# Output products of two late blocks in the banks of h, and another order of the tail

## The chip, the cores and the metric

The kernel runs on one core of one Trainium2 chip. The metric is the time of the device for one execution, in microseconds (us); a kernel is run several times and the median counts. The kernel before takes 222.48 us in the median of three runs (222.0 to 222.53). A profile comes from one further look at the hardware: it lists every instruction with its start, its duration, and what it waited for.

The engines are named as the profile names them: PE is the matrix engine (TensorE), PEld its loads of weights, DVE the vector engine, ACT the scalar engine, POOL GpSimd, and SP the queue from which most transfers are issued.

## The reference

Two layers follow each other. The first is attention in which a query sees only the keys of its own cluster; the second works on each token by itself.

```python
q_assign = argmax(q_n @ c_n);  k_assign = argmax(k_n @ c_n)      # 16 clusters per head
scores = where(q_assign == k_assign, q @ k.T / sqrt(64), -1e9)
x = softmax(scores) @ v                       # 4 batches, 8 heads, 768 tokens, 64 per head
# x is put together to 3072 tokens of 512
h = x @ w_in                                  # 512 -> 1024
solu = h * softmax(h)
ln = (solu - mean(solu)) / sqrt(var(solu) + 1e-6) * g_ln
out = ln @ w_out                              # 1024 -> 512, float32
```

## The kernel before

**Work and names.** The 3072 tokens are 24 blocks of 128, numbered f = 0 to 23. Attention comes first in each batch (products S and V, exponentials E, normalisation N); a block of the second layer may start as soon as its tokens' attention is done. The last blocks thus form the tail of the kernel, in which nearly all work is that of the second layer. For a block f the steps are these, and they are the names in the order of the work:

- `h{f}.{f2}.{part}` (PE, line 772): the products x @ w_in; half f2 of the 1024 columns goes to the bank `hb[f2]`. Block 23 alone splits them by three and one slices of x, so that one product of each half remains to be done when the last slice of x is there.
- `hm{f}.{f2}` (DVE, line 782): reads the bank, writes -h to the tile w_st and takes the minimum. It frees the bank.
- `ex{f}` (ACT, line 798): exp with the sum over the row. `u{f}` (POOL or DVE, line 805): the product of both. Block 23 does these in two halves.
- `tu{f}` (SP, line 811): transposes u by a transfer. Blocks 22 and 23 do it on PE instead: `ptu{f}.{f2}` (line 759) puts half f2 into the first bank of sb1 or sb0, and `tu{f}.{f2}` copies it from there to `uT`, half 0 on ACT (line 768) and half 1 on DVE (line 766). This uT lies in the tile w_g, which held w_out and is free by then.
- `bn{f}.{f2}`, `as{f}`, `ag{f}` (DVE, lines 816, 835, 821 and 823): statistics of u, small sums, and the variance. `al{f}` (POOL, line 840): its power of -1/2, alpha.
- `y{f}.{part}` (PE, line 844): eight products of uT with w_out (centred beforehand) into the bank `mb`, two to a part. Parts 0 and 1 need the first half of uT, parts 2 and 3 the second. Block 23 makes two halves of 256 columns, one in the second bank of sb0, one in the bank ob.
- `sc{f}` (ACT or DVE, lines 856 and 858): alpha times the bank, into a tile y of which there are two. It frees `mb`. `ou{f}` (SP, for one half of block 23 ACT's queue; line 868): the transfer to memory.

**Order.** All steps stand in one list, `ORDER`, written out by hand, from which the program is made: each engine runs its own steps in the sequence of that list, one after the other, and a step that waits holds up what stands behind it on its engine. The table `AWAY` moves single steps to another engine. Semaphores between engines are set by the framework from the tiles that instructions read and write; the two banks of sb0 are one tile to it. `take` and `give` in a step's entry only assert that a bank is free in the list's sequence.

**What the steps around the change wait for.** `y21` stands behind `sc20`, since both use `mb`; `y22` behind `sc21`. In the list of before, `sc20` comes ahead of `ex23`, and `h23.1.1`, the last product of the last h, comes behind the eight products of `y20`. DVE makes `bn22` before and after it reads the first half of h of block 23. `sc{f}` writes a tile y, so it also waits until the transfer of block f - 2 has landed.

**The start.** Before the first transposes of q and k, PE runs seven products on zeros (`idle_products`, line 946), which fill the time until the first loads land.

Of the kernel before, what the change touches and what calls it, by code (L numbers as in the profile page):

```python
# [10 lines left out]
F32 = mybir.dt.float32  # L11
# [8 lines left out]
AWAY.update(dict.fromkeys("""  # L20
    ca0.0.1.1.0 ca0.2.0.1 ca1.0.0.1 ca3.1.1.0 ca3.2.0.1 cv0.0.1 cv0.1.0 cv0.2.1 cv1.2.0
    cv1.3.1 cv2.0.1 cv2.1.0 cv3.0.0 cv3.0.1 cv3.3.0 pl0.0.0.1 pl0.0.1.0 pl0.1.1.1 pl2.2.1.0
# [113 lines left out]
ptx23.0 h22.1.1 V95.0 ou16 sc18 V95.1 hm22.1 N40 tx23.0 ag20 tu19 y19.0 y19.1 y19.2 ptx23.1 y19.3  # L136
tu20 ou17 tu21 ou18 ex22.0 h23.0.0 h23.1.0 tx23.1 as22 bn21.0 bn21.1 ag21 u22.0 al20 sc19 h23.0.1
y20.0 y20.1 y20.2 y20.3 sc20 hm23.0 bn22.0 h23.1.1 ptu22.0 ptu22.1 bn22.1 hm23.1 tu22.1 tu22.0
ex23.0 ex23.1 ou19 y21.0 y21.1 y21.2 y21.3 ou20 u23.0 u23.1 ag22 as23 ptu23.0 ptu23.1 tu23.1
bn23.0 bn23.1 ag23 al21 sc21 ou21 tu23.0 y22.0 y22.1 y22.2 y22.3 y23.1.0 y23.1.1 y23.1.2 y23.1.3  # L140
y23.0.0 y23.0.1 y23.0.2 y23.0.3 al22 sc22 al23 sc23.0 sc23.1 ou23.1 ou22 ou23.0
""".split()
# [31 lines left out]
def kernel(  # L174
# [15 lines left out]
    P = 128  # L190
# [509 lines left out]
    def y_of(f, x=None):  # L700

        return mb[:] if x is None else (ob, sb[0][:, 1])[x][:, parts_of(f, x)]

# [58 lines left out]

    def keep_u(f, f2):
        dst = ff[f, "uT"][:, f2 * (n_fc // 2):(f2 + 1) * (n_fc // 2), :]
        if f2:
            nc.vector.tensor_copy(dst, tail_bank(f"tu{f}.{f2}"))
        else:
            nc.scalar.copy(dst, tail_bank(f"tu{f}.{f2}"))
# [82 lines left out]
    def f_scale(f, e, x=None):  # L851
        if (f, "o") not in ff:
            ff[f, "o"] = mo.tile([P, d_model], F32, name="y")
        c = parts_of(f, x)
        if e == "ACT":
            nc.scalar.activation(ff[f, "o"][:, c], y_of(f, x), Act.Copy, scale=ff[f, "alpha"][:])  # L856
        else:
            nc.vector.tensor_scalar(ff[f, "o"][:, c], y_of(f, x), scalar1=ff[f, "alpha"][:],  # L858
                                    scalar2=None, op0=Alu.mult)
# [83 lines left out]
    def idle_products():  # L943

        for _ in range(7):
            nc.tensor.matmul(sb[0][:, 0], idle[:, :P], idle)
# [235 lines left out]
    for f in range(n_f):  # L1182
# [63 lines left out]
        if f"tu{f}.0" in by_pe:  # L1246
            for f2 in range(n_ff2):
                turned(f"tu{f}.{f2}", (lambda f=f, f2=f2: turn_u_pe(f, f2)), 0.3, s,
                       "DVE" if f2 else "ACT", (lambda f=f, f2=f2: keep_u(f, f2)),
                       [us[min(f2, nhv - 1)]] + [f"ce{fc}" for fc in range(n_fc)])  # L1250
# [27 lines left out]
        free = [f"ou{f - 2}"] if f >= 2 else [f"ce{fc}" for fc in range(n_fc)]  # L1278
        if f < n_f - 1:
            e = on(f"sc{f}", "ACT")  # L1280
            add(f"sc{f}", e, 0.585 if e == "ACT" else 0.65, s + 5, (lambda f=f, e=e: f_scale(f, e)),
                [f"y{f}.3", f"al{f}"] + free, prior("sc{}", f), give="m")
            add(f"ou{f}", "SP", 0.5, s + 8, (lambda f=f: f_out(f, nc.sync)), [f"sc{f}"], move=0.76)
            continue
# [70 lines left out]
```

## Time and profile before

| | us |
|---|---|
| median of three runs | 222.48 (222.0 to 222.53) |
| span of the profiled execution, first to last instruction | 220.5 |
| PE busy | 211.4 |
| DVE busy | 185.7 |
| ACT busy | 192.8 |
| POOL busy | 158.8 |
| PE busy within the last 13.5 us | 9.63 |
| DVE busy within the last 13.5 us | 8.76 |

The page gives no time of the profiled execution beside its span, so the runs' median stands 2.0 above it for what lies around the span. In a row of the time line the first number is the start, the second the duration; "x8" says that eight like instructions stand together, and the duration runs from the first's start to the last's end. Products overlap: one begins before the one ahead of it has its result. Brackets hold the idle time of the engine ahead of the row and what ended it. In the chain of waits each piece is followed back from the last instruction to what released it.

### The profile page before, as it was taken

To read this page: it belongs to the slowest core of one execution; us is meant where nothing else is said; L and a number is where in the kernel's file an instruction comes from. 1 tells how busy PE (TensorE), PEld (TensorE's weight loads), DVE (VectorE), ACT (ScalarE), POOL (GpSimd) and SP (SyncE) were. 2 spreads that over 40 slices of the span, in tenths; PEclk is the share of its full clock that TensorE was granted. 3 is DMA by queue.
4 is the path that set the end of the run, shared out by engine and by line. 5 is a ranking of instruction groups with operands and counts; after the bars stand their busy time and mean duration, and the time that the engine had idled before them with its cause. 6 is when DMAs were issued, how large, how long until landed. Compare 5 with 4: busy or idle time off the path is not lost.

```text
span 220.5 us, 6292 instructions
## 1 busy us (share of the span) xinstructions
PE 211.4 (96%) x2401; PEld 148.9 (68%) x2431; DVE 185.7 (84%) x430; ACT 192.8 (87%) x245; POOL 158.8 (72%) x198
## 2 busy tenths in 40 slices
PE   7899999999999999999999999999999999999984
PEld 4567577677678776777677677666777767655442
DVE  3699979968999999896799999994888856989982
ACT  3799999999999998999999989999999888685362
POOL 3686969897898999549939997879889054456610
PEclk9999999999999999999999999999999999999999
DMA  5998999999999993999999981939584229777522
GB/s 199 394 402 259 189 175 300 126 154 259 164 154 169 190 188 62 174 248 210 153 225 162 180 184 38 171 92 209 151 173 90 72 64 168 154 120 170 163 94 100
DMA packets 120911, 38.33 MB, mean 174 GB/s; under 512 B 109993, under 2 KB 116401, under 8 KB 120881
## 3 DMA queue, kind: packets, MB, share of 16 engines
q1 hardware_dynamic: 120448, 37.40, 81.7%
q10 hardware_dynamic: 432, 0.52, 0.7%
q8 instruction: 19, 0.31, 0.6%
q14 instruction: 12, 0.09, 0.2%
HBM read 23.11 MB, written 6.29 MB: 133 GB/s over the span
## 4 chain that ended last, share of the span: by engine, by line
PE 72%; DVE 10%; DMA 6%; POOL 5%; issue 3%; ACT 2%; SPq 1%; DVEq 0%; ACTq 0%; POOLq 0%
PE sb L641 22%; PE hb L772 16%; PE mb L844 15%; PE ob L663 12%; DMA w_st<-in_moe_w_in_dram 4%; PE hb L470 3%; DMA raw<-in_q_dram 2%; DVE w_st L782 2%; PE hb L396 2%; DVE xt L421 2%; DVE bs L816 2%; POOL kbig L441 1%; PE mb L470 1%; POOL w_in_sb L580 1%; POOL v L556 1%
## 5 line engine op out<-in xcount | busy, mean ns | idle before, releaser
L651 ACT ACTIVATE e<-sb 128x1024 bf16<-128x1024 f32 x144 | 139.9, 1024 | 8.9 <-PE sb L641 8.1
L641 PE MATMUL sb<-qbig,kbig 80*128 80x256 bf16 (+3 forms) x648 | 83.8, 261 | 1.3 <-ACT e L651 1.0
L641 PEld LDWEIGHTS <-kbig 80*128 80x128 bf16 (+1 forms) x648 | 62.9, 119 | 25.4 <-issue 8.6
L805 POOL TENSOR_TENSOR u<-e_sb,w_st 128x1024 bf16<-128x1024 bf16 x21 | 45.1, 2145 | 20.0 <-ACT e_sb L798 13.3
L663 PEld LDWEIGHTS <-e 128*128 128x128 bf16 x1152 | 48.6, 97 | 10.4 <-DVE x L686 0.6
L663 PE MATMUL ob<-v,e 128*128 128x65 bf16 x1140 | 51.4, 193 | 0.2
L772 PE MATMUL hb<-w_in_sb,xT 128*128 128x512 bf16 x173 | 50.6, 379 | 0.9 <-POOL v L1323 0.3
L844 PE MATMUL mb<-w_out_c,uT 128*128 128x512 bf16 x165 | 45.5, 379 | 1.2 <-DVE y L858 0.4
L816 DVE BATCH_NORM_STATS2 bs<-u 128x6 f32<-128x512 bf16 x48 | 31.6, 680 | 1.1 <-POOL u L805 1.1
L798 ACT ACTIVATE e_sb<-w_st,nmax 128x1024 bf16<-128x1024 f32 (+1 forms) x25 | 27.8, 1113 | 3.2 <-DVE w_st L782 1.8
L439 POOL CAST qbig<-xt 64x768 bf16<-64x768 f32 (+1 forms) x31 | 25.7, 830 | 6.5 <-PE ob L663 2.7
L441 POOL TENSOR_SCALAR kbig<-xt 64x768 bf16<-64x768 f32 (+1 forms) x32 | 27.6, 865 | 2.4 <-DVE xt L409 0.8
L840 POOL TENSOR_TENSOR alpha<-var,halves 128x1 f32<-128x1 f32 x24 | 15.3, 638 | 12.6 <-DVE var L823 8.0
L421 DVE STREAM_TRANSPOSE xt<-raw 128x768 f32<-128x768 f32 x24 | 22.5, 959 | 0.1
L844 PEld LDWEIGHTS <-uT 128*128 128x128 bf16 x176 | 15.2, 97 | 10.2 <-issue 0.8
L772 PEld LDWEIGHTS <-xT 128*128 128x128 bf16 x192 | 15.8, 98 | 8.8 <-issue 0.6
L686 DVE TENSOR_TENSOR x<-ob,den 128x256 bf16<-128x256 f32 (+2 forms) x40 | 19.0, 474 | 1.4
L782 DVE TENSOR_SCALAR_CACHE_REDUCE w_st<-hb 128x512 f32<-128x512 f32 x24 | 16.3, 680 | 3.8 <-PE hb L772 3.7
L782 DVE TENSOR_SCALAR_CACHE_REDUCE w_st<-hb,nmax 128x512 f32<-128x512 f32 x24 | 17.8, 740 | 1.9 <-PE hb L772 1.5
L856 ACT ACTIVATE y<-mb,alpha 128x512 f32<-128x512 f32 x15 | 10.3, 685 | 6.5 <-POOL alpha L840 3.6
L675 DVE RECIPROCAL den<-ob 128x4 f32<-128x4 f32 (+2 forms) x40 | 7.1, 178 | 10.4 <-PE ob L663 10.1
L556 POOL CAST v<-vf 128x384 bf16<-128x384 f32 x22 | 10.9, 504 | 3.3 <-DMA vf<-in_v_dram 2.6
(109 smaller groups left out, 202.6 us busy)
## 6 DMA issues: line engine op xcount, KB each, us to landing
vf<-in_v_dram SPq DMA_DIRECT2D x16, 384.0 KB, 5.3
out_dram<-y SPq DMA_DIRECT2D x23, 256.0 KB, 2.5
raw<-in_k_dram SPq DMA_DIRECT2D x26, 192.0 KB, 4.6
raw<-in_q_dram SPq DMA_DIRECT2D x24, 192.0 KB, 5.1
w_g<-in_moe_w_out_dram SPq DMA_DIRECT2D x4, 512.0 KB, 8.7
w_st<-in_moe_w_in_dram SPq DMA_DIRECT2D x4, 512.0 KB, 8.0
raw<-in_q_dram SPq DMA_DIRECT2D x3, 384.0 KB, 6.6
raw<-in_k_dram SPq DMA_DIRECT2D x3, 384.0 KB, 7.6
```

The costliest lines, as they stand in the source:

```text
L421: nc.vector.transpose(xts[b, p, i][:], raw_of(b, p, i))
L439: (nc.vector if e == "DVE" else nc.gpsimd).tensor_copy(dst, src)
L441: (nc.vector if e == "DVE" else nc.gpsimd).tensor_scalar(dst, src, scalar1=inv_C, scalar2=1.0, op0=Alu.mult, op1=Alu.mult)
L641: nc.tensor.matmul(reg[:, c:c + wd], kb[u, pp, side_of(h), keys], qb[u, pp, side_of(h), su * P:su * P + wd])
L651: nc.scalar.activation(es[r][:, :w], src, Act.Exp, scale=exp_scale, bias=-exp_scale)
L663: nc.tensor.matmul(ops_of(group_of[n])[:, s, :VW], es[r][:, c0:c0 + P], v1[index[b, pair_of(h)] % R][:, side_of(h), kt, :VW], start=(kt == ...
L772: nc.tensor.matmul(hb[f2][:], xTs[f][:, dc, :], w_in_sb[:, dc, f2 * BANK:(f2 + 1) * BANK], start=(dc == 0), stop=(dc == n_dc - 1))
L782: nc.vector.tensor_scalar(ff[f, "h"][:, f2 * BANK:(f2 + 1) * BANK], hb[f2][:], scalar1=-1.0, scalar2=nmax[:, f2 - 1:f2] if f2 else 3.0e38, ...
L798: nc.scalar.activation(ff[f, "e"][:, cols(f, f2)], ff[f, "h"][:, cols(f, f2)], Act.Exp, bias=ff[f, "nmax"][:, n_ff2 - 1:], scale=-1.0, acc ...
L805: (nc.vector if e == "DVE" else nc.gpsimd).tensor_tensor(ff[f, "u"][:, cols(f, f2)], ff[f, "e"][:, cols(f, f2)], ff[f, "h"][:, cols(f, f2) ...
L816: nc.vector.bn_stats(ff[f, "bs"][:, f2, :], ff[f, "u"][:, f2 * BANK:(f2 + 1) * BANK])
L844: nc.tensor.matmul(y_of(f, x), ff[f, "uT"][:, fc, :], w_out_c[:, fc, parts_of(f, x)], start=(fc == 0), stop=(fc == n_fc - 1))
```

## The change

- The products `y21` go into `hb[0]` and `y22` into `hb[1]`; `sc21` and `sc22` read them there.
- The list is another from `bn21.0` on. PE: `h23.0.1 h23.1.1 y20 ptu22 y21 y22.0 y22.1 ptu23 y22.2 y22.3 y23.1 y23.0`. DVE: `bn21 hm23.0 hm23.1 bn22.0 ag21 u23.0 u23.1 bn22.1 ag22 bn23.0 as23 tu23.1 bn23.1 ag23 sc23.0`. ACT: `sc19 ex23.0 ex23.1 tu22.0 tu22.1 sc20 tu23.0 sc21 sc22 sc23.1`. POOL and the transfers keep their sequence.
- `tu22.1` goes from DVE to ACT.
- The results of blocks 20 to 23 go into four slices of w_g instead of the two tiles y, and no longer wait for earlier transfers.
- Five idle products at the start for seven.

```diff
+    tu22.1 ca0.0.1.1.0 ca0.2.0.1 ca1.0.0.1 ca3.1.1.0 ca3.2.0.1 cv0.0.1 cv0.1.0 cv0.2.1 cv1.2.0
...
-tu20 ou17 tu21 ou18 ex22.0 h23.0.0 h23.1.0 tx23.1 as22 bn21.0 bn21.1 ag21 u22.0 al20 sc19 h23.0.1
-y20.0 y20.1 y20.2 y20.3 sc20 hm23.0 bn22.0 h23.1.1 ptu22.0 ptu22.1 bn22.1 hm23.1 tu22.1 tu22.0
-ex23.0 ex23.1 ou19 y21.0 y21.1 y21.2 y21.3 ou20 u23.0 u23.1 ag22 as23 ptu23.0 ptu23.1 tu23.1
-bn23.0 bn23.1 ag23 al21 sc21 ou21 tu23.0 y22.0 y22.1 y22.2 y22.3 y23.1.0 y23.1.1 y23.1.2 y23.1.3
-y23.0.0 y23.0.1 y23.0.2 y23.0.3 al22 sc22 al23 sc23.0 sc23.1 ou23.1 ou22 ou23.0
+tu20 ou17 tu21 ou18 ex22.0 h23.0.0 h23.1.0 tx23.1 as22 bn21.0 u22.0 al20 sc19 h23.0.1 h23.1.1
+bn21.1 hm23.0 y20.0 y20.1 y20.2 y20.3 hm23.1 ex23.0 bn22.0 ptu22.0 ptu22.1 ag21 al21 ex23.1 tu22.0
+u23.0 y21.0 y21.1 y21.2 y21.3 ou19 tu22.1 u23.1 sc20 y22.0 y22.1 ptu23.0 ptu23.1 bn22.1 ag22 tu23.0 ou20
+sc21 bn23.0 as23 tu23.1 y22.2 y22.3 ou21 al22 sc22 bn23.1 ag23 y23.1.0 y23.1.1 y23.1.2
+y23.1.3 y23.0.0 y23.0.1 y23.0.2 y23.0.3 al23 sc23.1 sc23.0 ou23.1 ou22 ou23.0
...
     def y_of(f, x=None):

+        if n_f - 3 <= f < n_f - 1:
+            return hb[f - n_f + 3][:]
         return mb[:] if x is None else (ob, sb[0][:, 1])[x][:, parts_of(f, x)]
...
-    def keep_u(f, f2):
+    def keep_u(f, f2, e):
         dst = ff[f, "uT"][:, f2 * (n_fc // 2):(f2 + 1) * (n_fc // 2), :]
-        if f2:
+        if e == "DVE":
             nc.vector.tensor_copy(dst, tail_bank(f"tu{f}.{f2}"))
...
-            ff[f, "o"] = mo.tile([P, d_model], F32, name="y")
+            ff[f, "o"] = (w_g[:, f - n_f + 6] if f >= n_f - 4 else
+                          mo.tile([P, d_model], F32, name="y"))
...
-        for _ in range(7):
+        for _ in range(5):
...
+            room = f"h{f - n_f + 3}" if f >= n_f - 3 else "m"
...
-                take=None if part else "m")
-        free = [f"ou{f - 2}"] if f >= 2 else [f"ce{fc}" for fc in range(n_fc)]
+                take=None if part else room)
+        free = [f"ou{f - 2}"] if 2 <= f < n_f - 4 else [f"ce{fc}" for fc in range(n_fc)]
```

More of the change, by code (lines that the diff above doesn't have):

```diff
@@ L20 @@
 AWAY.update(dict.fromkeys("""
-    ca0.0.1.1.0 ca0.2.0.1 ca1.0.0.1 ca3.1.1.0 ca3.2.0.1 cv0.0.1 cv0.1.0 cv0.2.1 cv1.2.0
+    tu22.1 ca0.0.1.1.0 ca0.2.0.1 ca1.0.0.1 ca3.1.1.0 ca3.2.0.1 cv0.0.1 cv0.1.0 cv0.2.1 cv1.2.0
     cv1.3.1 cv2.0.1 cv2.1.0 cv3.0.0 cv3.0.1 cv3.3.0 pl0.0.0.1 pl0.0.1.0 pl0.1.1.1 pl2.2.1.0
@@ L1248 @@
                 turned(f"tu{f}.{f2}", (lambda f=f, f2=f2: turn_u_pe(f, f2)), 0.3, s,
-                       "DVE" if f2 else "ACT", (lambda f=f, f2=f2: keep_u(f, f2)),
+                       on(f"tu{f}.{f2}", "DVE" if f2 else "ACT"),
+                       (lambda f=f, f2=f2: keep_u(f, f2, on(f"tu{f}.{f2}", "DVE" if f2 else "ACT"))),
                        [us[min(f2, nhv - 1)]] + [f"ce{fc}" for fc in range(n_fc)])
@@ L1281 @@
             add(f"sc{f}", e, 0.585 if e == "ACT" else 0.65, s + 5, (lambda f=f, e=e: f_scale(f, e)),
-                [f"y{f}.3", f"al{f}"] + free, prior("sc{}", f), give="m")
+                [f"y{f}.3", f"al{f}"] + free, prior("sc{}", f),
+                give=room)
             add(f"ou{f}", "SP", 0.5, s + 8, (lambda f=f: f_out(f, nc.sync)), [f"sc{f}"], move=0.76)
```

## The prediction

> **What bounds the kernel now.** I read the page first, then the chain of waits over the last 15 us, then the time line of that stretch engine by engine, and last the first ten microseconds, since the change touches only the end of the order and the idle products at its start.
>
> ```profile
> span 220.5 us, 6292 instructions
> PE 72%; DVE 10%; DMA 6%; POOL 5%; issue 3%; ACT 2%; SPq 1%; DVEq 0%; ACTq 0%; POOLq 0%
> ```
>
> TensorE carries 72% of the chain that ended last. Up to the first half of block 23's exponentials the order of work is the same in both kernels, so what counts is how the last 14 us hang together. The chain of waits there:
>
> ```profile
> 213.82 1.73 PE mb L844 x8
> 215.54 0.87 PE sb L844 x8
> 216.42 0.89 PE ob L844 x8
> 217.49 0.48 DVE y L858
> ```
>
> and TensorE's rows of the time line:
>
> ```profile
> 207.98 1.89 PE L844 MATMUL mb<-w_out_c,uT 128*128 128x512 bf16 x8
> 209.92 0.61 PE L759 MATMUL sb<-ident_b,u 128*128 128x128 bf16 x8
> 210.78 1.89 PE L844 MATMUL mb<-w_out_c,uT 128*128 128x512 bf16 x8 [0.25 <-ACT y L856]
> 212.71 0.40 PE L759 MATMUL sb<-ident_b,u 128*128 128x128 bf16 x4
> 213.42 0.40 PE L759 MATMUL sb<-ident_b,u 128*128 128x128 bf16 x4 [0.31 <-DVE u L805]
> ```
>
> The reader is to see that TensorE has three holes in a row of products that otherwise follow each other. Eight products into a bank take 1.73 from start to start (the chain), so 0.216 each; eight transposes with rows ending 0.61 after the first began, each 0.22 long, are 0.056 apart, so 0.45 for eight and 0.22 for four. From 209.92 the work is 0.45 + 1.73 + 0.22 + 0.22 + 1.73 + 0.87 + 0.87 = 6.09, and by the chain the last product's result is there at 217.30 (216.42 + 0.89), some 0.17 of it the tail of the last (a row of eight takes 1.89, their starts 1.73), so the starts fill 209.92 to 217.13 = 7.21. **The holes are 1.12**: 0.41 ahead of 210.78 (block 21 waits until ACT has emptied mb of block 20), 0.20 ahead of 212.71 and 0.48 ahead of 213.42 (the transposes of block 23 wait for the two halves of its u on DVE).
>
> **The change, part by part.** *Banks of h.* Blocks 21 and 22 put their output products into hb0 and hb1. These are free as soon as DVE has read block 23's h, and no longer wait for the scaling of the block before. Same shape, same kind of bank, so the 0.216 per product stays. *Order.* The last product of h of block 23 goes ahead of block 20's outputs (TensorE's sum is unchanged), DVE reads both halves of that h before it makes statistics of block 22, and ACT does the exponentials of block 23 before it scales block 20. What I need are DVE's and ACT's rows:
>
> ```profile
> 197.97 0.68 DVE L782 TENSOR_SCALAR_CACHE_REDUCE w_st<-hb 128x512 f32<-128x512 f32 x1
> 198.78 0.75 DVE L782 TENSOR_SCALAR_CACHE_REDUCE w_st<-hb,nmax 128x512 f32<-128x512 f32 x1
> ...
> 208.03 0.21 DVE L821 BATCH_NORM_AGGREGATE mv<-bs 128x2 f32<-128x12 f32 x1
> 208.35 0.27 DVE L823 TENSOR_SCALAR var<-es,esum,mv 128x1 f32<-128x1 f32 x1
> 208.54 0.68 DVE L782 TENSOR_SCALAR_CACHE_REDUCE w_st<-hb 128x512 f32<-128x512 f32 x1
> 209.14 1.28 DVE L816 BATCH_NORM_STATS2 bs<-u 128x6 f32<-128x512 bf16 x2
> ...
> 210.63 0.58 ACT L768 COPY w_g<-sb 128x512 bf16<-128x512 bf16 x1
> 211.00 0.09 DVE L782 DVE_READ_ACCUMULATOR w_st<-hb,nmax 128x1 f32 x1
> 211.12 0.72 ACT L798 ACTIVATE e_sb<-w_st,nmax 128x512 bf16<-128x512 f32 x1
> 211.97 1.40 DVE L805 TENSOR_TENSOR u<-e_sb,w_st 128x512 bf16<-128x512 bf16 x2 [0.54 <-ACT e_sb L798]
> 212.45 0.18 ACT L798 ACTIVATION_READ_ACCUMULATOR e_sb<-w_st,nmax 128x1 f32 x1
> ...
> 213.28 0.20 DVE L821 BATCH_NORM_AGGREGATE mv<-bs 128x2 f32<-128x12 f32 x1
> 213.52 0.27 DVE L823 TENSOR_SCALAR var<-es,esum,mv 128x1 f32<-128x1 f32 x1
> 213.71 0.15 DVE L832 TENSOR_TENSOR es<-esum 128x1 f32<-128x1 f32 x1
> 213.89 0.15 DVE L835 TENSOR_SCALAR es<-es 128x1 f32<-128x1 f32 x1
> 213.96 0.41 DVE L766 COPY w_g<-sb 128x512 bf16<-128x512 bf16 x1
> 214.29 1.27 DVE L816 BATCH_NORM_STATS2 bs<-u 128x6 f32<-128x512 bf16 x2
> 215.60 0.21 DVE L821 BATCH_NORM_AGGREGATE mv<-bs 128x2 f32<-128x12 f32 x1
> 215.85 0.27 DVE L823 TENSOR_SCALAR var<-es,es,mv 128x1 f32<-128x1 f32 x1
> 216.27 0.55 POOL L840 TENSOR_TENSOR alpha<-var,halves 128x1 f32<-128x1 f32 x1 [1.78 <-DVE var L823]
> 216.85 0.47 ACT L856 ACTIVATE y<-sb,alpha 128x256 f32<-128x256 f32 x1 [0.44 <-POOL alpha L840]
> 217.35 0.35 ACTq L868 DMA_DIRECT2D out_dram<-y  x1
> ```
>
> DVE in the new order, each step by its distance in these rows. The first half of h stands at 208.14 (its last product gives way to the next at 207.98, and the tail is 0.16), so its reading starts at 208.18; the second half follows 0.81 later (197.97 to 198.78) at 208.99 and gives its minimum after 0.67, at 209.66. Block 22's first statistics go there (0.60 as in the pair of 1.28 less 0.68): 210.26. Block 21's means, moved behind them, take 0.32 + 0.19 (208.03, 208.35, 208.54): 210.77. ACT begins the exponentials 0.12 after the minimum (211.00 to 211.12), at 209.78; the first u may start 0.85 after that (211.12 to 211.97), 210.63, so DVE is the later one: u of block 23 at 210.77 and some 0.61 later, 211.38 (ACT's second half is there at 209.78 + 1.51 = 211.29, from 212.45 + 0.18 less 211.12). Before, these stood at 211.97 and 212.67: **1.2 to 1.3 earlier**, which fills the second and third hole. Then 0.61 for u, 0.68 for block 22's second statistics and 0.03 to their means: 212.70; 0.24 and 0.19 (213.28, 213.52, 213.71): 213.13; block 23's first statistics 0.60: 213.73; the two small sums 0.18 + 0.07 (213.71, 213.89, 213.96): the copy of uT's second half at 213.98, done at 214.39 (214.37 before: it gains nothing, since three statistics are now ahead of it). Second statistics 0.33 later at 214.31, done 214.98; means and variance 0.03 + 0.25 + 0.27: 215.54; POOL's alpha 0.15 later: 215.69 to 216.24, against 216.82 before.
>
> TensorE in the new order. The last product of h moves ahead, so block 20's outputs start at 208.20, block 22's transposes still at 209.92, block 21's outputs at 210.37 with no hole (hb0 was read by 208.87; their uT is older than that: its load of weights waited for nothing before), block 22's first four at 212.10. They need uT's first half from ACT: behind the exponentials (211.29, less the 0.09 by which the next overlaps) a copy of 0.58, so 211.8; 0.3 to spare. The four transposes twice over, 212.96 to 213.41, with u long there; four more products: 214.27. Block 23's outputs then need the copy at 214.39; they go into the second bank of sb0 while that copy reads the first, but the program's dependences hold for the whole two-bank tile, so that the first of them waits, not the fifth (in before's program that wait stands at the same product, and costs nothing). Start 214.43: **one hole of 0.16**. Two times 0.87 and the tail of 0.17: results at 216.34, against 217.30: 0.96 earlier, which is 1.12 less 0.16.
>
> *The copy of uT's second half of block 22 goes to ACT*: 0.58 there, before block 20's scaling, which nobody waits for any more; off DVE 0.42. If ACT had no room, block 22's last four products (213.41) would wait; they have 1.1. *Results in an old copy of w_out*: the last four blocks write there, so the scaling drops its waits for earlier outputs to land. None of these waits ended last in before's trace, except that DVE took 0.19 from TensorE's last result (217.30) to 217.49, one wait after the other; with fewer of them I count 0.1. The writing itself: the nearest rows are the scalings of 256 columns, 0.47 on ACT and 0.48 on DVE; that another place makes them a fifth longer or shorter, 0.1, is as far as I go to both sides, and I take 0. *DMA issues*: six outputs on the same queues in the same order; those of blocks 20 to 22 go out later or closer together, and the last two nearly together: ACT's at 216.24 + 0.04 + 0.50 (216.85 to 217.35) = 216.78, SP's at 216.44 + 0.48 + 0.03 = 216.95, where they were 0.64 apart.
>
> ```profile
> 218.00 0.33 SPq L868 DMA_DIRECT2D out_dram<-y  x1
> ...
> out_dram<-y SPq DMA_DIRECT2D x1, 128.0 KB, 1.7
> ```
>
> The last one lands 1.7 after its issue, with the queue to itself. Beside another of 128 KB it may be held up: from nothing to the whole of their former distance less the new one (0.64 less 0.17 = 0.47); I take 0.25, the middle, as half of each transfer's time would overlap. Sum at the end: 218.00 less 216.95 = 1.05 gained, 0.25 given back: **0.8**.
>
> *Five idle products for seven.* The start:
>
> ```profile
> 1.19 3.17 PE L946 MATMUL sb<-w_in_sb 128*128 128x512 bf16 x7 [1.19 <-DVE halves L884]
> 5.43 0.81 PE L396 MATMUL ob<-ident_f,raw 128*128 128x128 f32 x3
> 6.36 0.55 PE L396 MATMUL sb<-ident_f,raw 128*128 128x128 f32 x3
> 7.38 0.52 PE L396 MATMUL hb<-ident_f,raw 128*128 128x128 f32 x3 [0.36 <-DMA raw<-in_q_dram]
> ...
> 2.11 5.13 DMA raw<-in_q_dram
> ```
>
> Seven took until 4.15 (3.17 less a tail of 0.2), 0.43 each; two fewer free TensorE 0.85 earlier. The cover is the load of q that lands at 7.25, on which the products at 7.38 wait and the chain runs: 0 for me; between 0 and 0.1 gained, if an earlier transpose helps a cast; were the loads not in the way, it would be 0.85.
>
> The sum is made on the profiled execution, whose page gives its span alone, 220.5; the runs have 222.48 in the median, 2.0 more, and I take these 2.0 as unchanged: 222.48 less 0.8 is **221.7**.
>
> **The rivals.** *Slower: TensorE gets up to speed later.* Three transposes take 0.81 at 5.43 and 0.55 at 6.36, without tails (0.2 to 0.17) 0.64 and 0.33: TensorE doubles its pace between them, after some 5 us of unbroken work. With five idle products there are short holes from 3.3 on while q and k land. If the doubling came 2 to 3 us later, the products of 6.36 to 9 would take twice as long, 2 us more, of which the waits at 7.38 and its like hide some 0.5: plus 1.5, and TensorE is hardly idle after that, so it stays. 222.48 - 0.8 + 1.5 = 223.2. For it: TensorE stands idle 0.85 longer before 6.36. Against: it keeps the fast pace through the wait ahead of 7.38, and five products and nine transposes still fill most of 1.2 to 6. It decides as soon as the row at 6.36 reads 0.81. The Trainium skill, "TensorE: Matmul & The Clock Gate", Part 1 and Part 4, says that full clock comes after about 3.4 us of sustained work by a free-running window, and that transposes do not count as work in the same way. By that the two products taken away are just what counted, the rule speaks against this edit, and the time would be this rival's. The trace leaves it open: the doubling came when only transposes had run since 4.15.
>
> *DVE becomes the bound.* The copy (214.39) and alpha (216.24) both hang on one unbroken row of DVE from 208.18 on, with 0.1 to spare at the end. If each of its 17 steps lost 0.03, the end would come 0.5 later: 222.2. For it: DVE works without a hole over 7 us, and nothing in the new order lets it catch up. Against: the distances are from the same instructions in such a row.
>
> *More is gained.* If the last transfers don't hold each other up and the hole of 0.16 is not there: 222.48 - 1.05 - 0.15 = 221.3.
>
> *It does nothing:* hb isn't free in time and block 21 still waits for block 20. Then only the DVE part gains, and 0.41 of the 0.8 is left in: 222.1. The reading at 208.87 against 210.37 speaks against it.
>
> **How the numbers follow.** Forecast 221.7: 0.55, its own range 221.4 to 222.1 by the bounds of the transfer (0 to 0.47) and a step or two of DVE. More gained, 221.3: 0.13. DVE the bound or hb not free, 222.1 to 222.2: 0.22. TensorE slow at the start, 223.2: 0.10. The range, 221.2 to 222.5, leaves the last out and a little of the ends. About 0.3%, 0.67 us, is what a measurement of this kernel can tell from no change (its runs lie 0.5 apart), so faster means below 221.81: most of the forecast (0.44) and all of the third rival: 0.57. Same: 0.11 of the forecast, the 0.22, and 0.01 of the slow start: 0.34. Slower: 0.09.
>
> **What would show it.** Right: block 21's products follow the transposes without a hole, into hb; DVE's u of block 23 begins near 210.8 (counted from an equal 206.5), TensorE's last product ends about 1.0 earlier, one short hole ahead of the products into sb, ended by DVE's copy; last two issues 0.2 apart. Wrong: a row of 0.81 at 6.4; a hole ahead of block 22's outputs ended by ACT; the last scaling waiting for alpha; over 2.2 from the last issue to its landing.

## The result and the profile after

The changed kernel takes 220.98 us in the median of six executions (220.44 to 224.75), the kernel before in the same comparison 222.06 (six, 221.97 to 222.53). The ratio is 0.9938, with a 95% interval of 0.9911 to 0.9964: faster by 0.6%, and 0.22 under the predicted range. One of the six, 224.75, counts as a slow execution: here and in the table below the medians hold every execution, and the ratios and intervals leave the slow ones out.

The first lines of the page, and of its share of the chain by engine, of the kernel after:

```profile
span 219.2 us, 6308 instructions
PE 74%; ACT 10%; DVE 9%; issue 2%; DMA 2%; POOL 0%; SPq 0%; DVEq 0%
```

The span is 1.3 shorter, and TensorE's share of the chain went from 72% to 74%. To see where the 1.3 lies, I split the execution at one instruction that both kernels have at the same place, DVE's last copy of a slice of x. What follows it I call the tail. Its row in the time line of before, and of after:

```profile
206.37 0.21 DVE L752 COPY xT<-sb 128x128 bf16<-128x128 bf16 x1
```

```profile
205.89 0.21 DVE L754 COPY xT<-sb 128x128 bf16<-128x128 bf16 x1
```

The tail went from 14.18 (220.55 less 206.37) to 13.35 (219.24 less 205.89): **0.83 shorter**. What is ahead of it is 0.48 shorter. First the tail. The chain of waits of after:

```profile
207.88 1.73 PE mb L846 x8
209.61 0.45 PE sb L761 x8
210.05 2.59 PE hb L846 x12
212.64 0.45 PE sb L761 x8
213.09 0.86 PE hb L846 x4
213.95 0.01 issue
213.97 1.03 PE sb L846 x8
215.00 0.89 PE ob L846 x8
```

It is an unbroken row of products: block 20's, the transposes of block 22, twelve products into the banks of h without a stop, the transposes of block 23, the last four of block 22, and block 23's. The three holes of before are gone. The one that is left, and the end, in the time line of after:

```profile
210.22 1.34 DVE L807 TENSOR_TENSOR u<-e_sb,w_st 128x512 bf16<-128x512 bf16 x2
212.93 1.03 PE L846 MATMUL hb<-w_out_c,w_g 128*128 128x512 bf16 x4
213.49 0.42 DVE L768 COPY w_g<-sb 128x512 bf16<-128x512 bf16 x1
213.97 1.03 PE L846 MATMUL sb<-w_out_c,w_g 128*128 128x256 bf16 x8
215.21 0.55 POOL L842 TENSOR_TENSOR alpha<-var,halves 128x1 f32<-128x1 f32 x1 [1.80 <-DVE var L825]
215.79 0.47 ACT L859 ACTIVATE w_g<-sb,alpha 128x256 f32<-128x256 f32 x1 [1.06 <-POOL alpha L842]
215.98 0.48 DVE L861 TENSOR_SCALAR w_g<-ob,alpha 128x256 f32<-128x256 f32 x1 [0.92 <-PE ob L846]
216.30 0.35 ACTq L871 DMA_DIRECT2D out_dram<-w_g  x1
216.50 0.33 SPq L871 DMA_DIRECT2D out_dram<-w_g  x1
```

and its page's row for that last issue, which ends with the time from issue to landing:

```profile
out_dram<-w_g SPq DMA_DIRECT2D x1, 128.0 KB, 1.9
```

Four products from 212.93, 0.216 each, reach to 213.80; the next start at 213.97, right behind DVE's copy (213.49 + 0.42 = 213.91): a hole of 0.17.

Now what is ahead of the tail. After:

```profile
1.19 2.31 PE L949 MATMUL sb<-w_in_sb 128*128 128x512 bf16 x5 [1.19 <-DVE halves L887]
7.28 0.52 PE L396 MATMUL hb<-ident_f,raw 128*128 128x128 f32 x3 [0.44 <-ACT xt L407]
...
41.80 1.02 PE L774 MATMUL hb<-w_in_sb,xT 128*128 128x512 bf16 x4
```

Before, around the same products of the first h:

```profile
41.72 1.04 POOL L580 CAST w_in_sb<-w_st 128x1024 bf16<-128x1024 f32 x1 [0.80 <-DMA w_st<-in_moe_w_in_dram]
42.81 0.38 PE L772 MATMUL hb<-w_in_sb,xT 128*128 128x512 bf16 x1 [0.33 <-POOL v L1323]
```

The start gives 0.10 (7.38 to 7.28), and the rest, 0.38, is one hole: in the execution of before, a piece of w_in landed late, POOL's cast waited 0.80 for it, and TensorE stood idle ahead of 42.81. In that of after it landed in time. No edit of the change touches that load, so the question for the experiments was whether these 0.48 belong to the change.

### The profile page after: what moved, and what is told of

Read it like the earlier page. It is cut to its first block, busy times and chain, and to the rows that moved or that the text cites. A ratio compares the mean times of both kernels' runs of the same rounds, so it can differ in the third digit from the quotient of the medians.

```text
span 219.2 us, 6308 instructions
## 1 busy us (share of the span) xinstructions
PE 211.8 (97%) x2429; PEld 148.0 (68%) x2429; DVE 185.0 (84%) x429; ACT 193.0 (88%) x246; POOL 159.0 (73%) x198
## 4 chain that ended last, share of the span: by engine, by line
PE 74%; ACT 10%; DVE 9%; issue 2%; DMA 2%; POOL 0%; SPq 0%; DVEq 0%
PE sb L641 22%; PE hb L774 17%; PE mb L846 15%; PE ob L663 12%; ACT e L651 7%; PE hb L470 3%; DMA raw<-in_k_dram 2%; DVE w_st L784 2%; DVE xt L421 2%; DVE bs L818 2%; PE hb L846 2%; ACT xt L407 1%; PE hb L396 1%; DVE x L686 1%; ACT v L554 1%
## 5 line engine op out<-in xcount | busy, mean ns | idle before, releaser
L807 POOL TENSOR_TENSOR u<-e_sb,w_st 128x1024 bf16<-128x1024 bf16 x21 | 45.0, 2144 | 19.3 <-ACT e_sb L800 13.1
L774 PE MATMUL hb<-w_in_sb,xT 128*128 128x512 bf16 x192 | 53.4, 379 | 0.0
L441 POOL TENSOR_SCALAR kbig<-xt 64x768 bf16<-64x768 f32 (+1 forms) x32 | 28.4, 890 | 2.3 <-DVE xt L409 0.7
L439 POOL CAST qbig<-xt 64x768 bf16<-64x768 f32 (+1 forms) x31 | 25.0, 807 | 5.9 <-PE ob L663 2.7
L556 POOL CAST v<-vf 128x384 bf16<-128x384 f32 x22 | 11.7, 542 | 4.2 <-DMA vf<-in_v_dram 3.6
L531 POOL COPY kbig<-oht 32x768 f32<-32x768 f32 (+2 forms) x14 | 9.9, 711 | 3.2 <-DVE oht L505 1.3
```

Of the source, the lines that this page charges most:

```text
L439: (nc.vector if e == "DVE" else nc.gpsimd).tensor_copy(dst, src)
L441: (nc.vector if e == "DVE" else nc.gpsimd).tensor_scalar(dst, src, scalar1=inv_C, scalar2=1.0, op0=Alu.mult, op1=Alu.mult)
L774: nc.tensor.matmul(hb[f2][:], xTs[f][:, dc, :], w_in_sb[:, dc, f2 * BANK:(f2 + 1) * BANK], start=(dc == 0), stop=(dc == n_dc - 1))
L807: (nc.vector if e == "DVE" else nc.gpsimd).tensor_tensor(ff[f, "u"][:, cols(f, f2)], ff[f, "e"][:, cols(f, f2)], ff[f, "h"][:, cols(f, f2) ...
```

## The experiments

Each of the kernels e1 to e15 was timed in five rounds beside the kernel before on the same chip: e1, e2, e3 and e8 on one chip, e4 to e7 on a second, e9 to e12 on a third, e13 to e15 on a fourth. "Tail" and "tail starts" are read from each kernel's profile as above.

| kernel | idle products | median (executions) | before | ratio, 95% interval | tail | tail starts |
|---|---|---|---|---|---|---|
| before | 7 | | | | 14.18 | 206.37 |
| after | 5 | 220.98 (6) | 222.06 | 0.9938, 0.9911 to 0.9964 | 13.35 | 205.89 |
| e1_five_idle | 5 | 222.53 (12) | 222.15 | 1.0023, 0.9999 to 1.0047 | 14.16 | 206.31 |
| e2_seven_idle | 7 | 221.64 (12) | 222.15 | 0.9974, 0.9959 to 0.9989 | 13.37 | 206.47 |
| e8_one_idle | 1 | 222.14 (12) | 222.15 | 1.0000, 0.9971 to 1.0030 | 13.38 | 207.04 |
| e3_banks_only | 7 | 222.18 (12) | 222.15 | 1.0001, 0.9983 to 1.0018 | 14.16 | 206.06 |
| e4_tiles_y | 5 | 222.09 (12) | 222.06 | 1.0000, 0.9979 to 1.0020 | 14.24 | 212.24 |
| e5_order_mb | 5 | 222.12 (11) | 222.06 | 1.0002, 0.9987 to 1.0016 | 14.39 | 205.80 |
| e6_copy_dve | 5 | 221.64 (12) | 222.06 | 0.9988, 0.9966 to 1.0010 | 13.61 | 206.30 |
| e7_sb1 | 5 | 221.28 (13) | 222.06 | 0.9956, 0.9938 to 0.9974 | 13.46 | 208.92 |
| e9_after_again | 5 | 221.58 (12) | 222.08 | 0.9980, 0.9953 to 1.0007 | 13.34 | 206.11 |
| e10_seven_again | 7 | 221.35 (11) | 222.08 | 0.9974, 0.9964 to 0.9984 | 13.36 | 206.41 |
| e11_sb1_seven | 7 | 221.45 (11) | 222.08 | 0.9975, 0.9962 to 0.9988 | 13.49 | 205.74 |
| e12_nine_idle | 9 | 221.40 (12) | 222.08 | 0.9972, 0.9961 to 0.9983 | 13.38 | 206.59 |
| e13_copy_act | 7 | 221.74 (12) | 222.34 | 0.9965, 0.9942 to 0.9988 | 13.68 | 206.34 |
| e14_copy_act_nine | 9 | 221.46 (12) | 222.34 | 0.9963, 0.9938 to 0.9989 | 13.71 | 205.34 |
| e15_after_third | 5 | 221.48 (12) | 222.34 | 0.9969, 0.9943 to 0.9996 | 13.37 | 206.39 |

### The idle products, and the size of the change

Five idle products alone, in the kernel before:

```diff
-        for _ in range(7):
+        for _ in range(5):
```

> The kernel before with five idle products for seven, and nothing else. Theory A (the two idle products are what moved the work ahead of the tail): about 0.5 us faster than before, 221.6 against 222.1, and no hole on TensorE ahead of the third product of block 0's h near 42.5 us (0.38 before). Theory B (that hole depends on when the loads of w_in land in one execution, whatever the kernel): no difference in time, within 0.2 us, and the hole may be there or not. In both the first products of q that wait for a load at 7.4 us move by 0.1 us at most.

Measured: 0.4 slower, at the edge of what can be told (the interval just holds no change), which neither theory had. The hole near 42.5 us is not there, and yet the tail starts at 206.31, where before's starts at 206.37. The first products of q that wait for a load stand at 7.71, 0.33 later than before and not 0.1, as that load came later. Five products by themselves gain nothing.

The changed kernel with seven of them, which is the tail's part alone:

```diff
-        for _ in range(5):
+        for _ in range(7):
```

> The changed kernel with seven idle products again, so the tail alone. Theory A: 0.87 us faster than before, 0.5 slower than the changed kernel (221.2). Theory B: as fast as the changed kernel, 1.0 to 1.3 faster than before. The tail itself, from the first product of block 23's h on, is the same as in the changed kernel within 0.1 us in both.

Measured: 0.5 under before, less than the 0.87 of theory A, the tail 13.37. The tail's shortening is there without the start's, and half of the 1.08 of the first comparison is not. The changed kernel with one:

```diff
-        for _ in range(5):
+        for _ in range(1):
```

> The changed kernel with one idle product for five. Theory (the start hangs on the loads, and TensorE's clock is up in time): within 0.2 us of the changed kernel, three transposes at 6.2 us take 0.55. Rival (TensorE needs the idle products to get up to speed): the three transposes near 6.2 us take 0.81, TensorE doubles its pace only 2 to 3 us later, and the time is 1 to 1.5 us longer than the changed kernel's.

Measured: the tail is short as well (13.38), but it starts at 207.04, and the time is that of before, with 3 of 12 executions more than 1 us above the median. The profile does not show that the missing idle products are the cause. Its first products of h start at 42.01, no later than the 42.31 of the run e15_after_third with five; the tail starts late behind the same hole as in before, and a larger one:

```profile
42.41 1.04 POOL L580 CAST w_in_sb<-w_st 128x1024 bf16<-128x1024 f32 x1 [1.41 <-DMA w_st<-in_moe_w_in_dram]
43.50 0.38 PE L774 MATMUL hb<-w_in_sb,xT 128*128 128x512 bf16 x1 [0.90 <-POOL v L1329]
```

So why one idle product gave the time of before stays open. To settle the size, the changed kernel was run again as it is, and with seven and nine:

> The changed kernel once more, beside the same with seven idle products on the same chip. Theory of the tail (the change is worth what its tail is worth, 0.83 between the two profiles, and the 0.48 by which the first profile of the changed kernel was also ahead before the tail is chance): 0.6 to 0.9 under before, median 221.2 to 221.5, and the tail, from DVE's copy of block 23's second half to the end of the span, 13.3 to 13.5. Rival, the start (five idle products gain 0.3 to 0.5 more once the tail is changed too): 1.0 to 1.2 under before, and 0.3 to 0.5 under the one with seven.

> The changed kernel with seven idle products, the same program as in the earlier run that came out 0.5 under before. Theory of the tail: 0.6 to 0.9 under before and within 0.2 of the one with five. Rival, the start: 0.5 under before, 0.3 to 0.5 slower than with five. A third reading, that five products let TensorE come to its fast pace late in some executions: the spread of its times is narrower than with five, under 1.3 from lowest to highest where those with five have 2 and more.

> The changed kernel with nine idle products. They run until about 5.0 us (1.19 and nine times 0.43), with q landing at 7.25 at the latest. Theory that these products stand behind the loads: no difference from seven, within 0.2. Theory that they decide when TensorE comes to its fast pace: the first three transposes of q or k stand at 0.55 instead of 0.81, the spread of the times is no wider than with seven, and no run lies 2 us above the lowest. Rival: nine hold up the transposes ahead of the first casts, 0.3 to 0.8 slower than seven.

Measured: 0.50, 0.73 and 0.68 under before. The 0.50 of the kernel as it is falls short of the 0.6 to 0.9 that the theory of the tail gave, and its interval still holds no change; the rival, the start, is further off, since five products came out slower than seven. And once more, in the last comparison:

> The changed kernel as it is, on another chip or at another time. If 1.08 under before, as at first, is its size: 220.9 to 221.1. If the tail of 0.6 to 0.8 is its size and the rest came of few executions: 221.3 to 221.6, with some executions 2 and more above the lowest.

Measured: 0.86 under. The three sets of the changed kernel thus differ, 1.08, 0.50 and 0.86, and all their 30 executions together have a median of 221.45 (220.44 to 224.75), against 222.11 for all 139 of before: **0.66, within the 0.6 to 0.9 that the theory of the tail gave**. With seven products, 23 executions have 221.50.

The third reading, of the spread, held for the changed kernel itself: its executions lie between 220.44 and 224.75 with five products, 220.91 and 222.08 with seven, 221.21 and 221.77 with nine. Over all kernels run, 13 of 90 executions with five products lie more than 1 us above the median of their set, 1 of 58 with seven, and 9 of the 139 of before, which has seven too. So the count of products is not the only cause. Another shows in the executions themselves: 4 of the 13 and 6 of the 9 list a mean granted clock of 0.948 to 0.992, where nearly all others list 0.997 or more. Without these, 9 of 86 are left with five, 1 of 58 with seven, and 3 of 133 of before. That five products spread the times more is thus likely. In the fastest executions five gain nothing that can be told: the changed kernel's best with five is 220.44 and with seven 220.91, but in the kernel before five gave 221.86 at best and seven 221.15 on the same chip.

What one of the nine looks like stands in the profile of the run e7_sb1 (below), which has five products and took 224.19, where its set's median is 221.28; its mean granted clock is 0.999. Its time line at the start:

```profile
9.90 1.54 PE L396 MATMUL hb<-ident_f,raw 128*128 128x128 f32 x6
12.17 2.02 PE L396 MATMUL hb<-ident_f,raw 128*128 128x128 f32 x9
14.90 0.55 PE L396 MATMUL hb<-ident_f,raw 128*128 128x128 f32 x3
```

and its table by stretches (the busy time of PE, PEld, DVE, ACT and POOL, then the granted clock, the DMA engines' share and GB/s):

```profile
10.50:14.00 3.50, 3.50 (x22) 2.20 (x20) 2.89 (x9) 2.31 (x6) 1.78 (x5) 1.00 1.06 401
```

The same two views of after:

```profile
8.19 0.87 PE L396 MATMUL hb<-ident_f,raw 128*128 128x128 f32 x6
```

```profile
10.50:14.00 3.50, 3.49 (x32) 2.37 (x31) 3.22 (x9) 3.25 (x8) 3.08 (x9) 1.00 1.06 403
```

Six transposes take 1.54 there and 0.87 here; the fast pace comes only between 12 and 15 us. TensorE is busy throughout this stretch in both, 3.50 and 3.49 of 3.50, and gets through 22 products instead of 32. The column of the granted clock reads 1.00 in both, so this pace is seen in the durations alone. The tail starts at 208.92, some 2.5 later than the usual 206.4. The profile of e4_tiles_y has the same start (1.54 for its six) and, from 14 us to the end, a granted clock of 0.95 besides; it took 228.26.

### The parts of the tail, one by one

The banks of h for blocks 21 and 22, on the list of before:

```diff
     def y_of(f, x=None):
+        if n_f - 3 <= f < n_f - 1:
+            return hb[f - n_f + 3][:]
```

> The kernel before with block 21's and 22's output products in the banks of h, order and all else as before. Theory (the holes on TensorE hang on DVE's u of block 23): block 21's products start 0.41 earlier, without the hole ahead of them, and the 0.41 comes back as a longer hole ahead of block 23's transposes (0.6 for 0.2), so no gain, 0.0 to 0.1 us. Rival (the banks alone are the gain): 0.4 us faster.

Measured: nothing gained, tail 14.16. TensorE's time line shows where it went:

```profile
212.40 0.40 PE L761 MATMUL sb<-ident_b,u 128*128 128x128 bf16 x4 [0.45 <-DVE u L807]
213.11 0.40 PE L761 MATMUL sb<-ident_b,u 128*128 128x128 bf16 x4 [0.31 <-DVE u L807]
```

The hole ahead of block 21's products is gone, and as much has been added ahead of the transposes of block 23, which still wait for u. The converse, the new order with blocks 21 and 22 in mb again (where `sc20` and `sc21` then have to stand ahead of `y21` and `y22`):

```diff
-        if n_f - 3 <= f < n_f - 1:
-            return hb[f - n_f + 3][:]
...
-bn21.1 hm23.0 y20.0 y20.1 y20.2 y20.3 hm23.1 ex23.0 bn22.0 ptu22.0 ptu22.1 ag21 al21 ex23.1 tu22.0
-u23.0 y21.0 y21.1 y21.2 y21.3 ou19 tu22.1 u23.1 sc20 y22.0 y22.1 ptu23.0 ptu23.1 bn22.1 ag22 tu23.0 ou20
-sc21 bn23.0 as23 tu23.1 y22.2 y22.3 ou21 al22 sc22 bn23.1 ag23 y23.1.0 y23.1.1 y23.1.2
+bn21.1 hm23.0 y20.0 y20.1 y20.2 y20.3 hm23.1 ex23.0 sc20 bn22.0 ptu22.0 ptu22.1 ag21 al21 ex23.1 tu22.0
+u23.0 y21.0 y21.1 y21.2 y21.3 ou19 tu22.1 u23.1 ptu23.0 ptu23.1 sc21 y22.0 y22.1 bn22.1 ag22 tu23.0 ou20
+bn23.0 as23 tu23.1 y22.2 y22.3 ou21 al22 sc22 bn23.1 ag23 y23.1.0 y23.1.1 y23.1.2
```

> The changed kernel with blocks 21 and 22 in mb again; for that block 20's scaling stands between the two exponentials of block 23, and block 21's ahead of block 22's products. Theory: TensorE waits 0.8 us ahead of block 21's products for block 20's scaling and 0.4 to 0.5 ahead of block 22's for block 21's; results at the end 1.0 us later than in the changed kernel, so about as slow as before but for the start. Rival (the order alone is the gain): within 0.3 us of the changed kernel.

Measured: the whole gain is lost (tail 14.39, 1.04 more than after). Its rows:

```profile
210.67 1.89 PE L844 MATMUL mb<-w_out_c,uT 128*128 128x512 bf16 x8 [0.70 <-ACT w_g L857]
213.39 1.89 PE L844 MATMUL mb<-w_out_c,w_g 128*128 128x512 bf16 x8 [0.39 <-ACT w_g L857]
```

Here u of block 23 is early and the waits are for the scalings that empty mb. **Neither part is worth anything without the other.**

The copy of block 22's second half back on DVE:

```diff
-    tu22.1 ca0.0.1.1.0 ca0.2.0.1 ca1.0.0.1 ca3.1.1.0 ca3.2.0.1 cv0.0.1 cv0.1.0 cv0.2.1 cv1.2.0
+    ca0.0.1.1.0 ca0.2.0.1 ca1.0.0.1 ca3.1.1.0 ca3.2.0.1 cv0.0.1 cv0.1.0 cv0.2.1 cv1.2.0
```

> The changed kernel with the copy of the second half of block 22's uT on DVE again. Theory (DVE's row of work sets the copy of block 23's uT and alpha): everything on DVE behind it comes 0.42 us later, the hole ahead of block 23's products into sb grows from 0.17 to 0.6, the end comes 0.4 us later. Rival (DVE has slack): no change.

Measured: tail 13.61, 0.26 more than after, and the hole ahead of block 23's products grows from 0.17 to 0.43 (four products of 0.216 from 213.34, then 214.64), ended by DVE; the theory is right in kind, with less than its 0.6 and 0.4. The median, 221.64, is not told apart from the changed kernel's, so the 0.26 rests on the two profiles. The row:

```profile
214.64 1.03 PE L846 MATMUL sb<-w_out_c,w_g 128*128 128x256 bf16 x8 [0.27 <-DVE w_g L768]
```

The results of the last four blocks in the two tiles y, as before:

```diff
-            ff[f, "o"] = (w_g[:, f - n_f + 6] if f >= n_f - 4 else
-                          mo.tile([P, d_model], F32, name="y"))
+            ff[f, "o"] = mo.tile([P, d_model], F32, name="y")
```

> The changed kernel with the last four results in the two tiles y again. Theory: the scalings of block 23 wait until block 21's output has landed (issued some 0.1 us after its scaling ends at 214.1, 2.1 to land: 216.2), so the last two begin at 216.2 for 215.8 and 216.0: 0.2 to 0.4 us slower than the changed kernel. Rival: the landing is early enough and nothing changes.

Measured: the time of before. In its profile both of the last scalings wait for a landing:

```profile
222.99 0.47 ACT L858 ACTIVATE y<-sb,alpha 128x256 f32<-128x256 f32 x1 [1.26 <-DMA out_dram<-y]
223.10 0.48 DVE L860 TENSOR_SCALAR y<-ob,alpha 128x256 f32<-128x256 f32 x1 [1.55 <-DMA out_dram<-y]
```

Its tail, 14.24, is 0.89 longer than after's, in an execution whose products were also some 4% slower (eight into a bank take 1.97 instead of 1.89, at a granted clock of 0.95). The waits alone can be told from that: from TensorE's last result to the start of the last scaling it takes 0.63 (222.47 to 223.10), in after 0.09 (215.89 to 215.98), so they cost 0.54, and not the 0.2 to 0.4 expected. The medians agree in direction: 222.09 against 222.06 for before, where after's sets lie 0.50 to 1.08 under. In the old order the prediction counted 0.1 for these waits, presumably because blocks 20 to 22 were spread out; the new order brings their scalings together, and then two tiles are too few.

### The last hole, and the landing

Block 23's first half in the second bank of sb1, so that DVE's copy out of sb0 holds up nothing:

```diff
-        return mb[:] if x is None else (ob, sb[0][:, 1])[x][:, parts_of(f, x)]
+        return mb[:] if x is None else (ob, sb[1][:, 1])[x][:, parts_of(f, x)]
```

> The changed kernel with one half of block 23's outputs in the second bank of sb1 for that of sb0, so that its first product does not wait for DVE's copy out of sb0. Theory: the hole of 0.17 us ahead of it is gone and TensorE ends 0.17 earlier; the last two transfers are then issued together and the last lands up to 0.2 later after its issue, so 0 to 0.15 us is left. Rival: alpha becomes the last thing waited for and nothing is left.

> The changed kernel with block 23's first half in the second bank of the other two-bank tile (no hole ahead of it) and seven idle products. By the earlier run of this bank with five products the hole of 0.17 goes and alpha, on GpSimd, takes its place as what the last scaling waits for: within 0.15 of the one with seven idle products and the old bank. Rival: alpha's wait there came of that one execution, which was disturbed at its start; then it gains the 0.17.

Measured, with five and with seven idle products: 0.78 and 0.63 under before, no different from the changed kernel. The tails are 13.46 and 13.49, slightly longer than after's 13.35, although the hole is gone (in the one with seven, four products of 0.216 from 212.78, and the next at 213.64). The end of the one with seven:

```profile
215.06 0.55 POOL L842 TENSOR_TENSOR alpha<-var,halves 128x1 f32<-128x1 f32 x1 [1.80 <-DVE var L825]
215.64 0.47 ACT L859 ACTIVATE w_g<-sb,alpha 128x256 f32<-128x256 f32 x1 [1.05 <-POOL alpha L842]
215.66 0.48 DVE L861 TENSOR_SCALAR w_g<-ob,alpha 128x256 f32<-128x256 f32 x1 [0.74 <-POOL alpha L842]
216.15 0.38 ACTq L871 DMA_DIRECT2D out_dram<-w_g  x1
216.17 0.33 SPq L871 DMA_DIRECT2D out_dram<-w_g  x1
```

and its page's row for the last issue:

```profile
out_dram<-w_g SPq DMA_DIRECT2D x1, 128.0 KB, 2.0
```

Counted from the tail's start, the last issue comes 0.18 earlier than after's (216.17 less 205.74 against 216.50 less 205.89), so the hole's 0.17 did reach it. Both last scalings now wait for alpha, as the rival of the first expectation had it, in the second run too; but alpha only bounds what more could be won. What takes the 0.17 away is the end: from the last issue to the end of the span it is 3.06, in after 2.74. By then the time from the last issue to the end of the span seemed to follow the distance of the last two issues: 2.55 at 0.64 (before), 2.74 at 0.20 (after), 3.06 at 0.02. To change that distance alone, the copy of block 23's second half went to ACT, which lets DVE make alpha earlier:

```diff
-    tu22.1 ca0.0.1.1.0 ca0.2.0.1 ca1.0.0.1 ca3.1.1.0 ca3.2.0.1 cv0.0.1 cv0.1.0 cv0.2.1 cv1.2.0
+    tu22.1 tu23.1 ca0.0.1.1.0 ca0.2.0.1 ca1.0.0.1 ca3.1.1.0 ca3.2.0.1 cv0.0.1 cv0.1.0 cv0.2.1 cv1.2.0
...
-u23.0 y21.0 y21.1 y21.2 y21.3 ou19 tu22.1 u23.1 sc20 y22.0 y22.1 ptu23.0 ptu23.1 bn22.1 ag22 tu23.0 ou20
-sc21 bn23.0 as23 tu23.1 y22.2 y22.3 ou21 al22 sc22 bn23.1 ag23 y23.1.0 y23.1.1 y23.1.2
+u23.0 y21.0 y21.1 y21.2 y21.3 ou19 tu22.1 u23.1 sc20 y22.0 y22.1 ptu23.0 ptu23.1 bn22.1 ag22 tu23.0 tu23.1 ou20
+sc21 bn23.0 as23 y22.2 y22.3 ou21 al22 sc22 bn23.1 ag23 y23.1.0 y23.1.1 y23.1.2
```

> The changed kernel with seven idle products, block 23's first half in the other two-bank tile, and the copy of the second half of block 23's uT on ACT, right behind that of the first half, instead of on DVE. DVE then comes to block 23's last statistics 0.35 earlier, alpha too, and ACT's last scaling no longer ends with DVE's: its output goes out some 0.35 ahead of the last one instead of 0.02. Theory that the last two transfers hold each other up (last issue to end of the span 2.55 with the issues 0.65 apart, 2.74 with 0.20, 2.85 with 0.13, 3.05 with 0.02): 2.65 here, the tail 13.1 instead of 13.49, and the time 0.3 to 0.4 under the same without this copy on ACT. Rival, alpha alone decided there: the wait for alpha ahead of the last scaling goes, worth 0.02, and the landing stays at 3.05. Second rival: ACT has no room, its scalings of blocks 21 and 22 push its last one back behind 215.6, and the order of the last two issues turns round with nothing gained.

> The same with nine idle products. Theory that more of them only narrow the spread: median within 0.15 of the one with seven, lowest to highest under 0.8. Rival: nine hold the transposes of q up, as their profile shows 0.8 later at 7.97; then 0.2 to 0.5 slower than seven.

Measured: the issues moved apart as meant, to 0.37 in both, but the end came 3.24 and 3.28 after the last issue, where 2.65 was expected, and the tails are 13.68 and 13.71 for 13.1. **That theory fell.** The times are 0.60 and 0.88 under before. With nine products the median is 0.28 under the one with seven, not within 0.15, and its executions spread over 1.76 (220.84 to 222.60), not under 0.8: here nine products did not narrow the spread, which was 1.21 with seven. The time line of the one with seven:

```profile
215.80 0.33 SPq L871 DMA_DIRECT2D out_dram<-w_g  x1
215.90 0.47 ACT L859 ACTIVATE w_g<-sb,alpha 128x256 f32<-128x256 f32 x1 [0.30 <-POOL alpha L842]
216.40 0.35 ACTq L871 DMA_DIRECT2D out_dram<-w_g  x1
```

its page's row for the last issue:

```profile
out_dram<-w_g SPq DMA_DIRECT2D x1, 128.0 KB, 2.4
```

and its table by stretches, with the DMA engines' share as the last number but one:

```profile
216.25:216.75 0.50, 0.00 (x0) 0.00 (x0) 0.48 (x1) 0.12 (x1) 0.00 (x0) 1.00 0.92 324
217.25:217.75 0.50, 0.00 (x0) 0.00 (x0) 0.00 (x0) 0.00 (x0) 0.00 (x0) 1.00 1.00 344
218.25:218.75 0.50, 0.00 (x0) 0.00 (x0) 0.00 (x0) 0.00 (x0) 0.00 (x0) 0.95 0.06 20
```

The same table of the kernel with the copy still on DVE and seven idle products:

```profile
216.00:217.00 1.00, 0.00 (x0) 0.00 (x0) 0.15 (x1) 0.12 (x1) 0.00 (x0) 1.00 0.28 102
217.00:218.00 1.00, 0.00 (x0) 0.00 (x0) 0.00 (x0) 0.00 (x0) 0.00 (x0) 0.92 0.78 262
```

ACT's second copy pushed its scalings of blocks 21 and 22 back by 0.5, and with them their two outputs of 256 KB; the later of them went out 0.97 ahead of the last (215.80), instead of 1.65 in after (the issue at 214.85). The DMA engines are then full at some 340 GB/s, without the pause that the other run has between 216 and 217 (over that microsecond their share is 0.95 here and 0.28 there). The four outputs, 768 KB, take 2.3 us at this rate, which is about the full stretch from 215.8 to 218.1; so the last transfers seem to queue behind those of blocks 21 and 22. That rests on the two profiles; no run moved these outputs alone. At the very end, from 218.25 on, the share is 0.06, which is that of one of 16 engines: it reads as if a single engine lagged behind the others by about half a microsecond. What makes it late stays open; on the DMA side the trace shows one packet of instructions between 216.5 and 217.3, within this busy stretch, which was not tried by itself. From the table of DMA queues for these 0.8 us (packets, MB, share):

```profile
q14 instruction: 1, 0.01, 3.3%
```

So none of these variants is told apart from the changed kernel, whose own three sets differ by as much, and none has a shorter tail.

## Why the prediction was right and wrong

**The tail, right in each step.** The forecast positions were counted from a tail that starts at 206.37; after's starts 0.48 earlier, so 0.48 is taken off each.

| step | forecast | measured |
|---|---|---|
| first u of block 23 begins | 210.29 | 210.22 |
| copy of uT's second half begins | 213.50 | 213.49 |
| hole ahead of block 23's products | 0.16 | 0.17 |
| TensorE's last result | 215.86 | 215.89 |
| alpha done | 215.76 | 215.76 |
| ACT's last issue | 216.30 | 216.30 |
| SP's last issue | 216.47 | 216.50 |
| wait ahead of the last scaling (0.19 before) | 0.1 | 0.09 |
| given back by the last landing (1.7 to 1.9) | 0.25 | 0.2 |
| gain of the tail | 0.8 | 0.83 |

Two slips of the working cost nothing. The three holes add up to 1.09, not 1.12. And the order of work is not the same up to block 23's exponentials, as the prediction's first paragraph says: it differs from `bn21.1` on, ahead of them, and the sums go by the new list.

**The base, wrong.** The step that failed is the one that put the sum on 222.48 and took everything ahead of the tail as equal. The 222.48 was a median of three; with three more executions it is 222.06, and over all 139 it is 222.11. That is 0.4 of the 0.7 by which 220.98 lies under 221.7. The other 0.3 belongs, as far as the profiles show, to what lies ahead of the tail, costed at 0 to 0.1: in the two profiles it differs by 0.48. This is a matter of the execution and not of the change. Over the profiles above whose start was a usual one the tail starts anywhere from 205.34 to 206.59, whatever the number of idle products from five to nine; and of the 17 profiles three have the hole behind the late load of w_in: before (TensorE idle for 0.33), e13_copy_act (0.32) and e8_one_idle (0.90), the last two of them changed kernels. The lower end of the range allowed for the terms of the change, not for this spread. With 222.11 less 0.8 the forecast would have been 221.3, and all executions of the changed kernel together have 221.45; its two later sets, 221.58 and 221.48, lie inside the predicted range, and only the first lies under it. Why those six came out half a microsecond lower stays open.

**Five idle products at 0: right for the median, for a reason that was too narrow.** The medians of the changed kernel, 221.45 with five and 221.50 with seven, bear the 0 out. The 0.10 at 7.28 is within what executions differ: outside the late starts that product begins at 6.98 to 7.71 with five and at 6.92 to 7.71 with seven. What was missed is that the count seems to change how far executions spread.

**The rivals.** TensorE late at its pace happens, but only in some executions: this rival was a matter of how often, not of whether. The rule of the Trainium skill that was set beside it ("TensorE: Matmul & The Clock Gate", Part 1) puts full clock after about 3.4 us of sustained work, give or take half a microsecond. With TensorE at work from 1.19 on in nearly all of them, five of the 17 profiles have the fast pace by 5.2 us, which agrees; ten have it only between 6 and 7.4, and two after 12, so the scatter here is far wider. DVE as the bound: it kept its forecast to 0.07, and the rival fell; with the copy back on DVE it does become the bound, at 0.26. That it does nothing because hb isn't free in time: fell, block 21's products follow the transposes without a hole. (The banks on the old order do nothing, but for another reason: u of block 23 is late there.) More gained because the last transfers do not disturb each other: fell, they do.

**The results in w_g, undervalued.** The prediction gave this edit 0.1. In the run without it the last two scalings wait for landings, which costs 0.54, and the time is that of before. The working priced the edit against the old order; in the new one it is needed. The total was still right, as that price was never paid.

**The two last transfers: size right, reason too narrow.** The prediction spoke of one beside the other. The run with the copy on ACT shows that the outputs of blocks 21 and 22 are on the way at the same time, and suggests that full DMA engines decide.

## What to carry to other kernels

Price an edit against the program in which it will stand, not against the one it is taken from: the banks alone are worth nothing, the change without the banks or without the new place of the results is worth nothing, and all together shorten the tail by 0.8. Before an absolute time is forecast, ask how far the part that the change does not touch moves from one execution to the next; here that spread is as large as the gain. A hole closed on the bounding engine is worth only what the last transfers let through.

## What the runs showed of the hardware that I had not expected

- TensorE's pace at the start can come some 7 us later than usual (six transposes 1.54 instead of 0.87, with TensorE busy 3.50 of the 3.50 us from 10.5 to 14), and the column of the granted clock, 1.00 there, does not show it.
- A small operation of POOL, 0.55 elsewhere, took 0.93 beside DVE's product of two tiles (210.22 to 211.56 above). Rows of after:

```profile
210.38 0.93 POOL L842 TENSOR_TENSOR alpha<-var,halves 128x1 f32<-128x1 f32 x1 [1.47 <-DVE var L825]
212.86 0.55 POOL L842 TENSOR_TENSOR alpha<-var,halves 128x1 f32<-128x1 f32 x1 [1.55 <-DVE var L825]
```

  The Trainium skill, "SBUF — State Buffer", section on the two separate sides, says that a GpSimd operation that reads SBUF and a DVE instruction with two inputs from SBUF lock each other out for a whole instruction; the row agrees in direction, with 0.38 more. It cost nothing here, as nobody waited for that alpha before 213.38.
- With the DMA engines full (shares of 0.92 and 1.00 above), the last output of 128 KB takes 2.4 from issue to landing, against 1.7 in before, and by the share of 0.06 at the end one of 16 engines is the last to finish.
